# A mixed attention and FFN kernel: the first up product moved to VectorE, the router's V group moved forward, silu by tanh, one down phase

## Chip, cores, metric

One core of one Trainium2 chip. The metric is the device time of one execution in microseconds (us), median over several executions. In the profiles PE is TensorE's matmuls, PEld its weight loads, DVE VectorE, ACT ScalarE, POOL GpSimd, SP the engine that issues most transfers. A ratio is the mean time of one kernel's runs over the mean of the other's of the same rounds, so it isn't quite the ratio of the medians that are quoted.

## The reference, cut to what matters

```python
# x: [1, 2048, 1024] bf16, wqkv: [1024, 3072], w_gate, w_up: [1024, 3584], w_down: [3584, 1024]
g = sigmoid((x * gate_w).sum(-1, keepdims=True))
# A: linear attention over 32 heads of 32
q, k, v = split(x @ wqkv);  phi(t) = where(t > 0, t + 1, exp(t)) + 1e-6
kv = einsum("bhsd,bhse->bhde", phi(k), v);  z = phi(k).sum(s)
a = (phi(q) @ kv / (phi(q) . z + 1e-6)) @ wo
# B: one row of x, chosen by a router, goes through a gated FFN
r = x @ w_r;  idx = argmax(r)
y = (silu(x[idx] @ w_gate) * (x[idx] @ w_up)) @ w_down * sigmoid(r[idx])
b = x;  b[idx] += y
return g * a + (1 - g) * b
```

The 2048 rows are 16 tiles of 128. The FFN is for a single row, so its 22 MB of weights are each used once: they can be multiplied on TensorE (the row as weights, padded to 32 columns) or row by row on VectorE (weights times a per-partition scalar, added up), with a column sum at the end.

## The kernel before

K and V of each tile are made as "units" of eight matmuls into one of four PSUM buffers. ScalarE and VectorE empty a K or Q unit (relu, exp, then the phi on VectorE), ScalarE alone empties a V unit. V is cut in three groups; the third ("router group", `vb == 2`) also carries the columns of the router and of the gate.

```python
    ps_work = ctx.enter_context(tc.tile_pool(name="ps_work", bufs=4, space=PSUM))
    ...
    # start: K of tiles 2 and 3, then the router group of V of all tiles
    for t in (2, 3):
        kv_open(t)
        for nb in range(2): ...            # K units
    for t in range(NT):
        unit_V(t, 2)
    ...                                    # router: maximum, its row, load of that row of x
    for t in range(4, NT):                 # tiles: K, K, V, V, one or two Q; FFN steps between
        for nb in range(4):
            unit_KV(t, nb)
            ...
        for i in range(Q_PER_T[t]):
            unit_Q(*q_units.popleft())
            ffn_slot(t, 4 + i)
    unit_Q(*q_units.popleft())
    for t in range(NT - 4, NT):
        unit_KVACC(t)
    down_finish()                          # column sum of the down rows, row of x stored
    gates()
    unit_Q(*q_units.popleft())
    unit_Q(*q_units.popleft())
    ...
    ph1.close()                            # gives back the pools of the first phase
    ...
    tmpb = ctx.enter_context(tc.tile_pool(name="tmpb", bufs=2))
    ps_den = ctx.enter_context(tc.tile_pool(name="ps_den", bufs=3, space=PSUM))
```

The end of the down phase, and the first user of memory that `ph1.close()` gives back:

```python
    def down_finish():
        ps = ps_ffn.tile([P, 256], F32, tag="f", name="yps")
        ...                                                    # 4 column sums on TensorE
        brow = rt.tile([P, 256], BF, name="brow")              # rt is a pool of the first phase
        dve.scalar_tensor_tensor(brow[:], ps[:], sig[:, 0:1], xsel4[:], op0=ALU.mult, op1=ALU.add)
        nc.gpsimd.dma_start(out=xp[bass.ds(nonlocal_idx[0], 1), :]..., in_=brow[0:128:32, :])

    def den_group(pair):
        dps = ps_den.tile([P, 512], F32, tag="d")
        ...                                                    # 16 matmuls
        dn = tmpb.tile([P, 512], F32, tag="dn")                # tmpb is a pool of the last phase
        act.activation(dn[:], dps[:], ACTF.Identity, bias=eps_t[:, 0:1])
        ...
```

## Time and profile before

| | before |
|---|---|
| time, us (median of 3) | 250.39 |
| span of the profiled run, us | 248.1 |
| first matmul of the unbroken stream, us | 7.28 |
| end of the matmuls on the chain of waits (eight small ones follow), us | 244.29 |
| TensorE without a matmul record between these two, us | 1.6 |
| VectorE busy | 65% |

The third to fifth rows say it all: from 7.28 on TensorE works without a break. (The 1.6 us are each stretch's length less TensorE's busy time in it, added up from 7.28 on.)

### The profile page before, as it was taken

The numbers are of one execution on the slowest core, as the hardware profiler recorded it, in microseconds if no ns is written. First come the engines' busy times: TensorE is split into PE (matmuls) and PEld (weight loads), VectorE is DVE, ScalarE is ACT, GpSimd is POOL, SyncE is SP. The second block draws the span as 40 slices with busy tenths as digits, with TensorE's granted clock in tenths as the row PEclk, the third lists the DMA queues.
The fourth block names the chain that finished last, engine by engine and source line by source line (L and its number), as shares of the span: only waits on it lengthen the run. The fifth ranks groups of instructions, "written<-read, shape, count | busy, mean of one in ns | idle before, by whom it ended". The sixth has DMA issues, their size and how long they took to land.

```text
span 248.1 us, 4887 instructions
## 1 busy us (share of the span) xinstructions
PE 241.3 (97%) x1925; PEld 123.8 (50%) x1947; DVE 162.4 (65%) x261; ACT 127.5 (51%) x215; POOL 51.9 (21%) x100
## 2 busy tenths in 40 slices
PE   8899999999999999999999999999999999999994
PEld 3446776654555554454655456444444444444442
DVE  0045112279993479996979972586878999953442
ACT  3087333356556265457266555568887633333210
POOL 6000000300000100000340000211666689940000
PEclk9999999999999999999999999999999999999999
DMA  6999998569963693899299973130000563455122
GB/s 186 309 261 214 232 389 274 172 192 355 344 213 85 191 312 96 263 321 340 99 294 314 439 266 130 47 107 1 0 3 12 170 223 129 167 169 152 62 85 85
DMA packets 46309, 47.76 MB, mean 193 GB/s; under 512 B 16776, under 2 KB 35472, under 8 KB 46224
## 3 DMA queue, kind: packets, MB, share of 16 engines
q1 hardware_dynamic: 45648, 46.28, 61.4%
q0 software_dynamic: 608, 1.19, 1.8%
q8 instruction: 15, 0.25, 0.4%
q14 instruction: 6, 0.05, 0.1%
q10 hardware_dynamic: 32, 0.00, 0.0%
HBM read 39.33 MB, written 8.39 MB: 192 GB/s over the span
## 4 chain that ended last, share of the span: by engine, by line
PE 84%; DVE 9%; DMA 4%; issue 1%; SPq 1%; DVEq 0%
PE ps L83 77%; DVE gacc L83 6%; PE first L83 3%; DMA wt<-in_B_w_down_dram 2%; DMA wkv<-in_A_wqkv_dram 2%; PE kvacc L83 2%; DVE eg L83 1%; DVE pk L83 1%; PE dps L83 1%; PE pm L83 1%; SPq L83 1%; PE gps L83 0%; DVE pq_all L83 0%; DVE ot L83 0%; DVE sg L83 0%
## 5 line engine op out<-in xcount | busy, mean ns | idle before, releaser
L83 PE MATMUL ps<-wkv,xT 128*128 128x352 bf16 (+2 forms) x604 | 106.4, 334 | 0.3
L83 PEld LDWEIGHTS <-xT 128*128 128x128 bf16 x640 | 62.3, 98 | 49.7 <-issue 0.9
L83 PE MATMUL ps<-xT,wq 128*128 128x512 bf16 x244 | 57.0, 379 | 1.0 <-issue 0.6
L83 ACT ACTIVATE u<-ps 128x512 f32<-128x512 f32 x60 | 35.8, 597 | 40.0 <-PE ps L83 38.1
L83 PE MATMUL ps<-m_sb,pq_all 128*128 128x512 bf16 (+2 forms) x259 | 55.3, 372 | 0.3
L83 ACT ACTIVATE e<-u 128x512 f32<-128x512 f32 x64 | 40.3, 630 | 2.0
L83 PEld LDWEIGHTS <-pq_all 128*128 128x128 bf16 x264 | 25.5, 98 | 30.2 <-issue 0.4
L655 POOL TENSOR_TENSOR pq_all<-pq_all,rb 128x512 bf16<-128x512 bf16 x32 | 36.5, 1161 | 14.4 <-DVE rb L83 13.9
L83 PEld LDWEIGHTS <-wq 128*128 128x128 bf16 x256 | 24.1, 98 | 28.7 <-issue 2.2
L83 DVE SCALAR_TENSOR_TENSOR gacc<-wt,hcol,gacc 128x1024 f32<-128x1024 bf16 x27 | 34.6, 1280 | 2.3 <-DMA wt<-in_B_w_down_dram 1.9
L83 DVE SCALAR_TENSOR_TENSOR ot<-ps,gate,xg 128x512 bf16<-128x512 f32 (+2 forms) x33 | 23.5, 721 | 15.1 <-PE ps L83 14.2
L83 DVE SCALAR_TENSOR_TENSOR pq_all<-ps,e 128x512 bf16<-128x512 f32 x32 | 21.8, 684 | 15.0 <-ACT e L83 14.9
L83 ACT ACTIVATE xg<-xt,omg 128x1024 f32<-128x1024 bf16 x16 | 18.1, 1145 | 25.9 <-DVE ot L83 25.9
L83 DVE SCALAR_TENSOR_TENSOR pk<-ps,e 128x512 bf16<-128x512 f32 x28 | 19.1, 687 | 8.1 <-ACT e L83 8.0
L83 DVE STREAM_SHUFFLE rb<-rdp 128x512 f32<-128x512 f32 x32 | 22.4, 726 | 0.0
L83 ACT CAST vt<-ps 128x352 bf16<-128x352 f32 x32 | 14.5, 453 | 13.9 <-PE ps L83 13.7
L213 POOL MEMSET vt<- 128x22 bf16 x16 | 3.0, 277 | 71.7 <-PE kvacc L83 71.2
L83 DVE SCALAR_TENSOR_TENSOR gacc<-wt,xs_f,gacc 128x2048 f32<-128x2048 bf16 x7 | 16.4, 2344 | 0.0
L83 ACT CAST vc<-ps 128x320 bf16<-128x320 f32 x16 | 6.8, 427 | 9.9 <-PE ps L83 9.9
L83 DVE COPY rg<-ps 128x2 f32<-128x2 f32 x16 | 2.5, 161 | 13.0 <-ACT vc L83 13.0
L355 POOL DMA_DIRECT2D xs<-in_A_x_dram x1 | 0.7, 711 | 41.8 <-DVE sig L83 41.8
L83 DVE SCALAR_TENSOR_TENSOR pk<-first,e 128x512 bf16<-128x512 f32 x4 | 2.8, 692 | 8.7 <-ACT e L83 8.7
(101 smaller groups left out, 101.0 us busy)
## 6 DMA issues: line engine op xcount, KB each, us to landing
wt<-in_B_w_down_dram SPq DMA_DIRECT2D x14, 512.0 KB, 5.2
wt<-in_B_w_gate_dram SPq DMA_DIRECT2D x8, 512.0 KB, 5.1
wt<-in_B_w_up_dram SPq DMA_DIRECT2D x8, 512.0 KB, 8.8
xt<-xp SPq DMA_DIRECT2D x16, 256.0 KB, 2.6
out_dram<-ot SPq DMA_DIRECT2D x15, 256.0 KB, 2.0
wt<-in_B_w_gate_dram SPq DMA_DIRECT2D x8, 384.0 KB, 7.0
wt<-in_B_w_up_dram SPq DMA_DIRECT2D x8, 384.0 KB, 7.0
wkv<-in_A_wqkv_dram SPq DMA_DIRECT2D x8, 256.0 KB, 5.3
```

What stands on the lines that cost most here:

```text
L83: inst = fn(*a, **k)
L213: nc.gpsimd.memset(vt_t[t][:, :, 32:33], 1.0)
L355: nc.gpsimd.dma_start(out=xs8[:], in_=x2d[bass.ds(idx_val, 1), :].rearrange("o (c p) -> (o c) p", p=P))
L655: nc.gpsimd.tensor_tensor(sl, sl, rb[:], op=ALU.mult)
```

## The change

The intent: take the 32 matmuls of the first half's up product off TensorE, which is full, and give them as eight rows to VectorE, which isn't. To make room there, silu drops two slow reciprocals for a tanh, the router is settled sooner, so that its rows can start sooner, and all down rows stand in one phase at the end. Cut to its core:

```diff
-Q_PER_T = {4: 2, 5: 1, 6: 1, 7: 2, 8: 1, 9: 1, 10: 2, 11: 1, 12: 1, 13: 1, 14: 1, 15: 0}
+Q_PER_T = {4: 2, 5: 1, 6: 1, 7: 2, 8: 2, 9: 1, 10: 2, 11: 1, 12: 1, 13: 1, 14: 1, 15: 1}
-GATE_STEPS = {...}  # gate rows in tiles 4 to 7
+REDUCE_AFTER = {(6, 3): 0, (9, 4): 1}
+ROW_STEPS = {...}   # gate rows in tiles 3 to 5, up rows in tiles 6 to 9
-DOWN_STEPS = {8: ..., 15: (1, 1, 1)}
+DOWN_STEPS = {10: (0, 0, 0, 1, 1, 1), 11: (1, 1, 1, 1, 1), ... 15: (1, 1, 1, 1, 1)}
     ...
     for c in range(1, KC):
         load_k(c)
+    sp.dma_start(out=wkv[:, :, v_cut : 2 * D], ...)            # router group of V
     for t in (2, 3):
         sp.dma_start_transpose(out=xT[:, :, t * P : (t + 1) * P], ...)
-    sp.dma_start(out=wkv[:, :, v_cut : 2 * D], ...)
     ...
-    sp.dma_start(out=wq[:], in_=wqkv_v[:, :, 0:D])            # now behind the router's row
     ...
-    for t in (2, 3):
-        ...                                                    # K units of tiles 2 and 3
+    for t in range(3):
+        unit_V(t, 2, ps_t, "t")
+    unit_V(3, 2)
     ...
-    for t in range(NT):
+    for t in range(4, NT):
+        if t in (4, 12):
+            unit_KV(2, (t - 4) // 8)
         unit_V(t, 2)
     ...
     def finish_gate(half, ps, w):
-        act.activation(eg[:, 0:w], ps[:, 0:w], ACTF.Exp, scale=-1.0)
-        dve.tensor_scalar_add(eg[:, 0:w], eg[:, 0:w], 1.0)
-        dve.reciprocal(eg[:, 0:w], eg[:, 0:w])
-        dve.tensor_tensor(sg[:, 0:w], ps[:, 0:w], eg[:, 0:w], op=ALU.mult)
+        act.activation(sg, ps[:, 0:w], ACTF.Tanh, scale=0.5)
+        dve.scalar_tensor_tensor(sg, sg, 1.0, ps[:, 0:w], op0=ALU.add, op1=ALU.mult)
     ...
-        yield from g0
-        yield from u0
+        for wi, wmat in enumerate((B_w_gate, B_w_up)):
+            yield from half0_rows(wmat)
+            yield from gate_up(1, (wi,))
     ...
     for t in range(NT - 4, NT):
         unit_KVACC(t)
-    down_finish()
     gates()
     unit_Q(*q_units.popleft())
     unit_Q(*q_units.popleft())
+    down_finish()
```

More of the change, by code (lines that the diff above doesn't have):

```diff
@@ L32 @@
 N_WARM = 6
-Q_PER_T = {4: 2, 5: 1, 6: 1, 7: 2, 8: 1, 9: 1, 10: 2, 11: 1, 12: 1, 13: 1, 14: 1, 15: 0}
+Q_PER_T = {4: 2, 5: 1, 6: 1, 7: 2, 8: 2, 9: 1, 10: 2, 11: 1, 12: 1, 13: 1, 14: 1, 15: 1}
 VH = (11, 11, 10)
-GU_AFTER = {(7, 3): 8, (9, 3): 8, (11, 3): 8}
-KV_AFTER = {(7, 3): (4, 5, 6), (11, 3): (8, 9, 10)}
-KV_LAST = {(7, 3): 7, (11, 3): 11}
-FLUSH_AFTER = {(8, 3), (12, 1)}
-GATE_STEPS = {4: (0, 1, 0, 1, 0, 1), 5: (0, 0, 1, 0, 1), 6: (0, 1, 0, 1, 0), 7: (1,)}
+REDUCE_AFTER = {(6, 3): 0, (9, 4): 1}
+KV_AFTER = {(7, 3): (4, 5, 6, 7), (11, 3): (8, 9, 10, 11)}
+FLUSH_AFTER = {(10, 2)}
+ROW_STEPS = {4: (0, 1, 0, 1, 0, 1), 5: (0, 1, 0, 1, 1), 6: (0, 0, 0, 0, 1), 7: (0, 1, 1, 0, 1), 8: (0, 1, 0, 1, 1), 9: (1,)}
 M_AFTER = {3: (0, 0), 6: (0, 1), 9: (1, 0), 12: (1, 1)}
-DOWN_STEPS = {8: (0, 0, 0, 0, 1), 9: (1, 1, 1), 10: (0, 1, 1, 1, 1, 1), 11: (1, 1, 1), 12: (1, 1, 1, 1, 1), 13: (1, 1, 1, 0, 1), 14: (1, 1, 1, 0, 1), 15: (1, 1, 1)}
+DOWN_STEPS = {10: (0, 0, 0, 1, 1, 1), 11: (1, 1, 1, 1, 1), 12: (1, 1, 1, 1, 1), 13: (1, 1, 1, 1, 1), 14: (1, 1, 1, 1, 1), 15: (1, 1, 1, 1, 1)}
 FFN_DEPTH = 10
-NORM_PER_T = [3, 2, 0, 2, 2, 2, 2, 2, 2, 2, 2, 0, 0, 0, 0, 0]
+NORM_PER_T = [3, 3, 0, 2, 2, 2, 2, 2, 2, 2, 2, 1, 0, 0, 0, 0]
 @with_exitstack
@@ L76, with in_order @@
     strict = [True]
-    def in_order(engine, names):
+    strict_dve = [False]
+    def in_order(engine, names, own=(False,)):
         last = [None]
@@ L83, in call @@
                 inst = fn(*a, **k)
-                if last[0] is not None and strict[0]:
+                if last[0] is not None and (strict[0] or own[0]):
                     tc.add_manual_dep(inst.ins, last[0].ins.name, NOSYNC, reason="program order on this engine")
@@ L94 @@
     dve = in_order(nc.vector, ["memset", "tensor_copy", "tensor_scalar", "tensor_scalar_add", "tensor_tensor", "scalar_tensor_tensor",
-                               "reciprocal", "max", "max_index", "tensor_reduce", "stream_shuffle"])
+                               "reciprocal", "max", "max_index", "tensor_reduce", "stream_shuffle"], strict_dve)
     sp = in_order(nc.sync, ["dma_start", "dma_start_transpose"])
@@ L140 @@
         load_k(c)
+    v_cut = D + 32 * (VH[0] + VH[1])
+    sp.dma_start(out=wkv[:, :, v_cut : 2 * D], in_=wqkv_v[:, :, D + v_cut : 3 * D])
     for t in (2, 3):
         sp.dma_start_transpose(out=xT[:, :, t * P : (t + 1) * P], in_=x2d[t * P : (t + 1) * P, :])
-    v_cut = D + 32 * (VH[0] + VH[1])
-    sp.dma_start(out=wkv[:, :, v_cut : 2 * D], in_=wqkv_v[:, :, D + v_cut : 3 * D])
     for g4 in range(1, 4):
@@ L221, in kv_evac, with unit_V @@
         phi_dve(ps[:], phi_exp(ps[:]), pk_t[t][:, 512 * nb : 512 * nb + 512])
-    def unit_V(t, vb):
+    def unit_V(t, vb, pool=ps_work, tag="w"):
         h0, nh = sum(VH[:vb]), VH[vb]
         n = 32 * nh + (2 if vb == 2 else 0)
-        ps = ps_work.tile([P, 512], F32, tag="w")
+        ps = pool.tile([P, 512], F32, tag=tag)
         for c in range(KC):
@@ L292 @@
         phi_evac(first[1][nb][:], pk_t[1][:, 512 * nb : 512 * nb + 512])
-    for t in (2, 3):
-        kv_open(t)
-        for nb in range(2):
-            pool, tag = (ps_t, "t") if t == 2 else (ps_work, "w")
-            ps = pool.tile([P, 512], F32, tag=tag)
-            kv_mm(ps, t, nb, 0, KC)
-            kv_evac(ps, t, nb)
+    for t in range(3):
+        unit_V(t, 2, ps_t, "t")
+    unit_V(3, 2)
     ps_t_cm.__exit__(None, None, None)
@@ L314 @@
     dve.tensor_copy(r_bf[:], rg[:, 0, :])
-    unit_V(0, 0)
+    unit_KV(3, 0)
     rps = ps_ffn.tile([16, P], BF, tag="f")
@@ L369 @@
     h_bf = [rt.tile([P, 512], BF, name=f"h_bf{i}") for i in range(2)]
-    sg = rt.tile([P, 512], F32)
+    sg_t = [rt.tile([P, 512], F32, name=f"sg{i}") for i in range(2)]
     ffn_state = {}
@@ L390, in finish_gate, with h_transpose @@
     def finish_gate(half, ps, w):
-        eg = tmp.tile([P, 512], F32, tag="ffn_e", bufs=1)
-        act.activation(eg[:, 0:w], ps[:, 0:w], ACTF.Exp, scale=-1.0)
-        dve.tensor_scalar_add(eg[:, 0:w], eg[:, 0:w], 1.0)
-        dve.reciprocal(eg[:, 0:w], eg[:, 0:w])
-        dve.tensor_tensor(sg[:, 0:w], ps[:, 0:w], eg[:, 0:w], op=ALU.mult)
-    def finish_up(half, ps, w):
-        dve.tensor_tensor(h_bf[half][:, 0:w], ps[:, 0:w], sg[:, 0:w], op=ALU.mult)
-        def h_transpose():
-            hps = ps_ffn.tile([P, 16], F32, tag="f")
-            nb = w // P
-            for b in range(nb):
-                pe.matmul(hps[:, 4 * b : 4 * b + 4], lhsT=h_bf[half][:, b * P : (b + 1) * P], rhs=sel4[:], start=True, stop=True)
-            dst = hcol[:].rearrange("p (j b) -> p j b", b=7)[:, :, 4 * half : 4 * half + nb]
-            src = hps[:, 0 : 4 * nb].rearrange("p (b j) -> p j b", j=4)
-            dve.tensor_copy(dst, src)
-        ffn_state["pending"] = h_transpose
+        sg = sg_t[half][:, 0:w]
+        act.activation(sg, ps[:, 0:w], ACTF.Tanh, scale=0.5)
+        dve.scalar_tensor_tensor(sg, sg, 1.0, ps[:, 0:w], op0=ALU.add, op1=ALU.mult)
+    def finish_up(half, ps, w):
+        dve.scalar_tensor_tensor(h_bf[half][:, 0:w], ps[:, 0:w], 0.5, sg_t[half][:, 0:w], op0=ALU.mult, op1=ALU.mult)
+    def h_transpose():
+        hps = ps_ffn.tile([P, 28], F32, tag="f")
+        for b in range(7):
+            half, col = b // 4, P * (b % 4)
+            pe.matmul(hps[:, 4 * b : 4 * b + 4], lhsT=h_bf[half][:, col : col + P], rhs=sel4[:], start=True, stop=True)
+        dve.tensor_copy(hcol[:].rearrange("p (j b) -> p j b", b=7), hps[:].rearrange("p (b j) -> p j b", j=4))
     def gate_up(half, which):
@@ L427, in compute, with half0_rows @@
                     if c == KC - 1:
-                        if half == 0:
-                            ffn_state["up0"] = lambda: finish_up(half, ps, w)
-                        else:
-                            (finish_gate, finish_up)[wi](half, ps, w)
+                        (finish_gate, finish_up)[wi](half, ps, w)
                 yield load, compute
-    def gate_rows():
+    def half0_rows(wmat):
         for c in range(KC):
             def load(c=c):
-                return gate_up_load(0, B_w_gate, c)
+                return gate_up_load(0, wmat, c)
             def compute(wt, c=c):
@@ L447, in gate_rows, with rows_reduce @@
             yield load, compute
-    def gate_reduce():
-        ps = ps_red.tile([P, 512], F32, name="gps")
+    def rows_reduce(wi):
+        ps = ps_red.tile([P, 512], F32, tag="red", name=f"red{wi}")
         for j in range(4):
@@ L453, in gate_reduce @@
                       start=True, stop=True, tile_position=(0, 32 * j))
-        finish_gate(0, ps, 512)
-        ffn_state["up0"]()
+        (finish_gate, finish_up)[wi](0, ps, 512)
     def down_rows():
@@ L497, in ffn_pieces @@
     def ffn_pieces():
-        g0, u0, gu, dn = gate_rows(), gate_up(0, (1,)), gate_up(1, (0, 1)), down_rows()
-        yield from g0
-        yield from u0
-        for n in (2, 4):
-            yield from islice(dn, n)
-            yield from islice(gu, 8)
-        yield from dn
+        for wi, wmat in enumerate((B_w_gate, B_w_up)):
+            yield from half0_rows(wmat)
+            yield from gate_up(1, (wi,))
+        yield from down_rows()
         yield from wo_pieces()
@@ L515, in ffn_prefetch @@
             inflight.append((nxt[0](), nxt[1]))
-    def ffn_flush():
-        pend = ffn_state.pop("pending", None)
-        if pend is not None:
-            pend()
     def ffn_step(n):
@@ L554 @@
     q_units = deque((g, j) for j in range(4) for g in range(NG))
-    for t in range(4):
-        for vb in range(2):
-            if (t, vb) != (0, 0):
-                unit_V(t, vb)
+    unit_KV(3, 1)
     ffn_prefetch(2)
@@ L565, with reduce_at @@
     ffn_prefetch(4)
+    strict_dve[0] = True
     router_part1()
-    first_after[5] = xsel_ld[0]
+    wq_ld = nc.sync.dma_start(out=wq[:], in_=wqkv_v[:, :, 0:D])
+    queue_order(wq_ld)
+    tc.add_manual_dep(wq_ld.ins, xsel_ld[0].ins.name, SYNC, reason="small transfers ahead of the weights")
     ffn_prefetch()
     for t in range(4):
+        for vb in range(2):
+            unit_V(t, vb)
+            if (t, vb) == (3, 0):
+                router_part2()
+            if t == 3:
+                ffn_step(1)
+    for t in range(4):
         unit_KVACC(t)
+    def reduce_at(t, i):
+        if (t, i) in REDUCE_AFTER:
+            rows_reduce(REDUCE_AFTER[(t, i)])
+            ffn_step(8)
     def ffn_slot(t, i):
-        gs, ds = GATE_STEPS.get(t, ()), DOWN_STEPS.get(t, ())
+        gs, ds = ROW_STEPS.get(t, ()), DOWN_STEPS.get(t, ())
         if i < len(gs):
@@ L581 @@
             unit_KV(t, nb)
-            if (t, nb) == (4, 0):
-                router_part2()
             for t0 in KV_AFTER.get((t, nb), ()):
                 unit_KVACC(t0)
-            ffn_step(GU_AFTER.get((t, nb), 0))
-            if (t, nb) == (7, 3):
-                gate_reduce()
-            if (t, nb) in KV_LAST:
-                unit_KVACC(KV_LAST[(t, nb)])
+            reduce_at(t, nb)
             if (t, nb) in FLUSH_AFTER:
-                ffn_flush()
+                h_transpose()
             ffn_slot(t, nb)
@@ L595 @@
             unit_Q(*q_units.popleft())
+            reduce_at(t, 4 + i)
             ffn_slot(t, 4 + i)
+    strict_dve[0] = False
     unit_Q(*q_units.popleft())
```

## The prediction

> **What bounds the kernel now.** I read the page's busy shares first, then the stretches by time, then the waits of TensorE, then single rows of the time line where the change cuts in. The shares and the clock:
>
> ```profile
> span 248.1 us, 4887 instructions
> PE 241.3 (97%) x1925; PEld 123.8 (50%) x1947; DVE 162.4 (65%) x261; ACT 127.5 (51%) x215; POOL 51.9 (21%) x100
> PEclk9999999999999999999999999999999999999999
> ```
>
> TensorE is 97% busy at full clock and VectorE 65%. A busy TensorE may still run below its peak, so I check by stretch (us, then busy time of PE, PEld, DVE, ACT, POOL, clock, DMA share, GB/s):
>
> ```profile
> 0.00:7.28 7.28, 5.51 (x29) 2.59 (x29) 1.02 (x3) 2.45 (x3) 3.96 (x39) 1.00 0.73 206
> 7.28:13.95 6.67, 6.62 (x30) 3.01 (x31) 0.00 (x0) 1.01 (x2) 0.00 (x0) 1.00 1.04 272
> 13.95:39.50 25.55, 25.55 (x170) 16.27 (x167) 8.65 (x27) 14.76 (x31) 0.00 (x0) 1.00 1.13 291
> ...
> 84.00:121.50 37.50, 37.33 (x352) 19.67 (x353) 33.63 (x37) 21.38 (x38) 0.65 (x4) 1.00 0.80 243
> ```
>
> From 7.28 on there is no stretch in which TensorE is not full. In the chain of waits 49 matmuls of 512 columns take 10.74 us, 0.219 each; 56 of 352 columns take 8.46, 0.151 each. For 84 to 121.5 the units between are worth 37.7 us at these rates, which is the whole stretch: although the chain of waits runs through VectorE there, TensorE loses nothing by it. TensorE's own waits, all of them:
>
> ```profile
> PE warm_ps L83 <- PEq L741: 1.0, 1, 1.0
> PE first L83 <- DMA wkv<-in_A_wqkv_dram: 0.7, 1, 0.7
> PE ps L83 <- issue: 0.6, 4, 0.2
> ```
>
> So the time is: 7.3 us of start, 237 us of matmuls end to end (7.28 to 244.29), 3.8 us of tail. **The only gains to be had are fewer TensorE microseconds; the only losses are new waits on TensorE.** Start (the first K chunk) and tail are not touched.
>
> **What the Trainium skill says.** (1) "TensorE: Matmul & The Clock Gate", Part 3 on packing small matmuls by row and column tiling: matmuls on different column strips run concurrently. The trace agrees: the up product of the first half is 32 matmuls of 512 columns that take 1.74 us, 54 ns each, a quarter of 219. So removing 32 of 1925 matmul records removes little. (2) "VectorE: DVE Perf Modes", the perf-mode tier table: a one-source tensor_scalar may reach a higher tier than a two-source tensor_tensor with fp32, for which it gives 2293 ns at 2048 elements. The trace has 1286 ns for the one-source row and 2344 for the accumulating rows, in line. (3) "ScalarE: Activation LUTs", Table sets: exp and tanh lie in one set, so tanh should bring no table load; the trace of before has one load (1283 ns), and the instruction list of the changed kernel has one too. (4) "DMA: Bandwidth & Descriptors", Latency and other measured facts: an effective 261 GB/s for a transposing DMA. In the trace the transposes of tiles 4 to 7 and 12 to 15 land at 21.4 and 29.3 us (below), 2 MB (tiles 8 to 15) in 7.9 us, 265 GB/s: it agrees.
>
> **Part 1: up product on VectorE.** What goes and what comes on TensorE:
>
> ```profile
> 79.95 0.91 PE kvacc L83 x96
> 80.86 1.74 PE ps L83 x32
> 82.61 0.85 PE gps L83 x7
> ```
>
> The middle piece (1.74 us) goes; a second column sum in fp32 like the third (0.85 us) comes. Net -0.89 us. The transposes of h are the same seven matmuls. On VectorE:
>
> ```profile
> L83 DVE SCALAR_TENSOR_TENSOR gacc<-wt,xs_f,gacc 128x2048 f32<-128x2048 bf16 x7 | 16.4, 2344 | 0.0
> L83 DVE RECIPROCAL eg<-eg 128x512 f32<-128x512 f32 x1 | 3.4, 3354 | 0.0
> L83 DVE RECIPROCAL eg<-eg 128x384 f32<-128x384 f32 x1 | 2.5, 2545 | 0.0
> L83 DVE TENSOR_SCALAR gacc<-wt,xs_f 128x2048 f32<-128x2048 bf16 x1 | 1.3, 1286 | 0.0
> ```
>
> Seven more rows of 2.344 and one of 1.286 are +17.7 us. Silu by tanh takes away both reciprocals (3.35 + 2.55) and both additions of one (0.43 + 0.35), -6.7 us; the fused multiplies replace plain ones of like size. Net +11.0 us: VectorE goes from 162.4 to about 173.4 us (70%).
>
> Does it still fit? Per token tile TensorE needs two K units (1.75 each), two V units (1.21 each) and the Q units (1.75 each): 7.7 us with one Q, 9.4 with two. VectorE's pitch is read from the time line of 93 to 104 us: a phi 0.60, a down row behind a phi 1.20, behind another row 1.30.
>
> - Tiles 4, 7 and 8 (two Q, three gate or up rows): 4 x 0.60 + 3 x 2.3 = 9.3 against 9.4 us. Tile 5 (one Q): 1.8 + 6.9 = 8.7 against 7.7, but tile 6, with one row, gives the time back, and the order has both K phis of a tile ahead of its rows.
> - The sums of the rows stand at the ends of tiles 6 and 9. Followed row by row, the last row ends within a few tenths of the time that TensorE arrives there. I count 0.1 us.
> - Tiles 12 to 15 (one Q, five down rows): 3 x (0.60 + 1.20) + 2 x 1.30 = 8.0 against 7.7 us. Before, tiles 13 to 15 had four, four and three rows. VectorE falls behind by 0.3 us a tile, some 1.2 us at the end. With four PSUM buffers for these units, I find the phi that must free the buffer of the next Q about 1 us ahead of its use in tile 15. The last sum of the down rows now stands behind three Q units, so the lag doesn't reach it. I count 0.
>
> **Part 2: the router group of V first.** Before, tiles 2 and 3 did their K units (7.0 us) at 13.95, then the 16 router units of V (1.09 us each). Now V of tiles 0 to 3 comes at 13.95, one K pair's first half follows, and tile 4's V. The work is the same, but the transposed x is wanted sooner: for tile 4 at 13.95 + 4 x 1.09 + 1.75 = 20.1 us instead of 25.3. It lands so (start and length of the issue; then the time to landing of that issue, and of the one for tiles 12 to 15):
>
> ```profile
> 11.97 5.82 SPq L83 DMA_TRANSPOSE xT<-in_A_x_dram  x1
> ...
> xT<-in_A_x_dram SPq DMA_TRANSPOSE x1, 9.4
> ...
> xT<-in_A_x_dram SPq DMA_TRANSPOSE x1, 6.5
> ```
>
> That is 11.97 + 9.4 = 21.4 us for tiles 4 to 7, and 22.79 + 6.5 = 29.3 for 12 to 15. The V chunk moves ahead of the small transposes, but the same bytes stand ahead of this one, and the DMA share is full, so I expect 20.5 to 21.3: **a new wait of about 0.7 us**. The next groups are wanted at about 25.2 and 31.4 us and should be there. The V chunk itself was issued at 11.34 and took 4.9 us; issued at about 6.0, it should land by about 13.5, just ahead of its use at 13.95.
>
> The router result comes some 1.8 us sooner (its transpose at about 37.7 instead of 39.5 us); the selected row of x took 10.5 us from there (39.5 to 50.0), so it lands at about 48.2, where TensorE arrives at about 48.0: 0.15 us. Wq now waits for that row: it used 28.5 to 39.7 us before, mostly behind other loads; 2 MB alone at the 389 GB/s that the page shows in its slice from 31 to 37 us are 5.4 us, so it lands near 56 against a first use at 56.5. I count 0.1.
>
> **Part 3: one down phase, two more Q units early, down sum last.** The work is the same. The 5.6 us DMA wait for down weights in the middle of the old chain disappears, which TensorE didn't feel. The last M product now stands directly ahead of the output stage; its copies have about 3 us, and are wanted in about 3: 0.1 us.
>
> **Sum.** -0.89 + 0.7 + 0.1 + 0.15 + 0.1 + 0.1 = +0.26 us: 250.39 + 0.26 = 250.6. As the schedule was visibly tuned around these edges, and each small wait counted can be zero, I take 250.3.
>
> **Rivals.**
> (a) *No new wait is felt*: the transposes land by 20.1. For it: in before the V chunk was mixed into them. Against it: the DMA is full up to there. Time: 250.4 - 0.9 = 249.5.
> (b) *VectorE becomes the bound of tiles 11 to 15*: if each row cost its mean duration without overlap (0.68 a phi, 1.28 a row), a tile would take 8.45 against 7.7, the lag would be 3 to 4 us by tile 15, and the Q units and the sum would wait some 1.5 us. Against it: the overlap is in the time line. Time: 252.
> (c) *Wq is late*: weights issued ahead of it and the row's landing push it by 2 us, straight onto the first Q unit. For it: it is 2 MB with half a microsecond of margin. Time: 252 to 252.5.
> (d) *The freed router time is worth a lot*: no. Nothing on TensorE waited for it before.
>
> **Range and chances.** The floor is 250.4 - 0.9 - 0.6 (the waits named issue), 248.9; (b) and (c) together make 253.5. Eight in ten: 249.0 to 252.2. Two per cent faster would be 245.4, for which TensorE has not the work to lose: 0.01. Two per cent slower is 255.4, which needs two of the rivals at their worst: 0.03. Within: 0.96.
>
> **What would show it.** TensorE busy near 240.4 us; VectorE near 173; the pair (column sums) twice at 0.85; a wait of V on the transposed x near 20 us of some 0.7; no wait of TensorE for VectorE over 0.5 us in tiles 11 to 15; the first Q unit without a wait on Wq; one table load. I am wrong if a wait on VectorE or on Wq of over 1 us stands among TensorE's waits, or if the start of the matmuls moves from 7.28.

## The result, and the profile after

253.44 us (median of 4 runs, 253.17 to 254.03) against 250.29 in the same rounds: ratio 1.0127, 95% interval 1.0101 to 1.0153. The same within 2%, but 3.1 us slower than predicted, and outside the predicted range.

The shares of the changed kernel:

```profile
span 251.8 us, 4856 instructions
PE 241.7 (96%) x1897; PEld 123.6 (49%) x1923; DVE 172.5 (69%) x264; ACT 127.5 (51%) x215; POOL 51.8 (21%) x100
```

VectorE came out as worked out (172.5 us against 173.4 predicted). 26 of TensorE's matmul records are missing here, so its sum is rough. Three of its stretches (start and end, length, then busy time of PE, PEld, DVE, ACT, POOL, clock, DMA share, GB/s):

```profile
13.40:36.95 23.55, 22.86 (x153) 14.67 (x152) 7.16 (x25) 12.40 (x27) 0.00 (x0) 1.00 1.05 246
...
124.50:163.60 39.10, 38.63 (x328) 20.02 (x336) 37.98 (x43) 22.64 (x40) 4.51 (x10) 1.00 0.60 199
163.60:191.20 27.60, 25.45 (x213) 10.95 (x210) 19.54 (x37) 20.71 (x39) 10.36 (x12) 1.00 0.11 35
```

The largest hole, 2.15 us, lies between 163.6 and 191.2, right behind the phase that was reordered, where the kernel before has 0.42 in a like stretch, all of it holes of missing records:

```profile
156.00:192.00 36.00, 35.58 (x266) 15.28 (x273) 27.18 (x56) 28.07 (x50) 15.08 (x16) 1.00 0.09 28
```

From the first matmul of the stream to the last, TensorE is without a record for 5.3 us in the changed kernel, 1.6 in the kernel before. TensorE's waits in the changed kernel, in order of size (us in total, times, longest):

```profile
PE pt L83 <- ACT dn L83: 1.8, 1, 1.8
...
PE ps L83 <- issue: 0.8, 5, 0.2
PE ps L83 <- DMA xT<-in_A_x_dram: 0.6, 1, 0.6
PE kvacc L83 <- issue: 0.4, 1, 0.4
PE ps L83 <- POOL pq_all L642: 0.3, 1, 0.3
PE ps L83 <- DMA wq<-in_A_wqkv_dram: 0.3, 1, 0.3
```

(The line left out is the warm-up's, 1.0 us in both kernels.) Not all of this is real. The profile of this run has 1897 matmul records, a later one of the same kernel (`after_again`) all 1923; that of the kernel before has 1925, with 1947 weight loads. In the chain of waits of this run, the last 51 us of matmuls come in pieces of 49 with a hole behind each:

```profile
210.88 0.05 issue
210.94 10.74 PE ps L83 x49
```

In that of `after_again` they are one piece:

```profile
196.40 51.49 PE ps L83 x240
```

So these holes are missing records. The five holes of 0.2 us named `issue` are of the same kind: no profile with all its records has them. The hole of 0.4 at `kvacc` isn't: all 128 matmuls of that group are there. Its cause the profile doesn't show, and no other profile has it.

Waits on xT and on Wq were in the prediction's list, and one at the output stage too, though for the copies of the last M product; here it is GpSimd's normalised `pq`. The first wasn't in the list: TensorE's product `pt` waits for ScalarE's `dn`. The chain of waits of the changed kernel around that place says why:

```profile
163.03 0.57 PE yps L83 x8
163.60 0.96 PE dps L83 x16
164.57 2.48 DMA xp<-brow
...
167.44 0.69 ACT dn L83
...
168.17 0.29 PE pt L83 x30
```

`dn` empties the denominators that `dps` made, which were there at 164.6; it starts at 167.4, when the store of `brow` has landed. The two have nothing to do with each other but memory: `brow` is in a pool of the first phase, `dn` in a pool of the last, and the second takes what the first gives back, so `dn` must wait until the store has read. (Which addresses overlap the profile doesn't show. The memsets of `rdp`, the first writes to the last pools' memory, wait for the store too, in both kernels: they start at 167.2 here and at 159.2 before.) And `pt` must wait for `dn`, because its four banks are the three of `ps_den` and one more, and `dps` holds one of the three. The time line of ScalarE in the kernel before has the same instruction without a wait, since there the store was issued at 157.4 and landed 1.7 us later, at 159.1, before `dps` was done (160.2):

```profile
160.38 0.67 ACT L83 ACTIVATE dn<-dps,eps_t 128x512 f32<-128x512 f32 x1
```

So the dependency isn't new. The change moved its release onto the path. Two theories for the 3 us, then. **Memory**: moving the down sum behind the Q units brings out the wait for `brow`'s store, and the smaller waits on transfers at the start make the rest. **Load**: VectorE, with 10 us more to do, runs late (it is 97% busy from 124.5 to 163.6), and what shows as waits is its delay.

### The profile page after: what moved, and what is told of

It reads as the page before. It is cut to its first block, busy times and chain, and to the rows that moved or that the text cites. A ratio compares the mean times of both kernels' runs of the same rounds, so it can differ in the third digit from the quotient of the medians.

```text
span 251.8 us, 4856 instructions
## 1 busy us (share of the span) xinstructions
PE 241.7 (96%) x1897; PEld 123.6 (49%) x1923; DVE 172.5 (69%) x264; ACT 127.5 (51%) x215; POOL 51.8 (21%) x100
## 4 chain that ended last, share of the span: by engine, by line
PE 77%; DMA 11%; SPq 3%; DVE 2%; issue 2%; ACT 1%; POOL 0%; POOLq 0%; DVEq 0%; ACTq 0%
PE ps L83 73%; DMA wq<-in_A_wqkv_dram 4%; DMA xT<-in_A_x_dram 3%; SPq L83 3%; DMA wkv<-in_A_wqkv_dram 2%; PE kvacc L83 2%; DMA xsel<-in_A_x_dram 1%; DMA xp<-brow 1%; PE red L83 1%; PE dps L83 1%; DVE pq_all L83 1%; SPq L537 1%; DMA c<-cand 1%; DVE rb L83 1%; ACT e L83 1%
## 5 line engine op out<-in xcount | busy, mean ns | idle before, releaser
L83 DVE SCALAR_TENSOR_TENSOR gacc<-wt,xs_f,gacc 128x2048 f32<-128x2048 bf16 x14 | 32.8, 2345 | 0.2
L83 DVE RECIPROCAL rd<-dn 128x512 f32<-128x512 f32 x2 | 6.7, 3353 | 3.2 <-POOL rdp L603 3.2
```

Source lines behind the costliest of these rows:

```text
L83: inst = fn(*a, **k)
```

## The experiments

### e1: memory of its own for brow

```diff
-        brow = rt.tile([P, 256], BF, name="brow")
+        brow = keep.tile([P, 256], BF, name="brow")
```

> The changed kernel, with the row that the down sum stores (brow) in memory that nothing reuses. Theory: the largest loss (TensorE's 1.8 us wait of pt for ACT dn) comes from dn taking memory that brow gives back, so that it must wait for brow's store to land, and the down sum is now so late that this landing is on the path. Then the wait goes and the time falls by 1.5 to 2.1 us, to about 251.5. Rival: VectorE's lag behind the down rows delays everything at that place; then the time stays within 0.4 us of 253.4.

252.09 us (251.82 to 252.54), ratio to before 1.0079 (1.0053 to 1.0105), against 1.0127 and, on another chip, 1.0171 of the changed kernel: 1.2 to 2.3 us less. (The changed kernel was not run in the rounds of e1 to e4, so these comparisons go by the ratios to the kernel before.) TensorE's wait at `pt` is gone; those on xT and Wq are longer in this profile (1.0 and 0.7 instead of 0.6 and 0.3), which hides some of the gain. ScalarE's time line:

```profile
164.74 0.69 ACT L83 ACTIVATE dn<-dps,eps_t 128x512 f32<-128x512 f32 x1 [0.26 <-PE dps L83]
```

`dn` now waits for `dps` alone. VectorE has exactly the same work as in the changed kernel, so its load isn't the cause of this wait. The time line says the same: in the changed kernel VectorE began `brow` at 163.80, 0.2 us after the down sum (163.60). The memory theory holds.

### e2: the kernel before, with the down sum last

```diff
-    down_finish()
     gates()
     unit_Q(*q_units.popleft())
     unit_Q(*q_units.popleft())
+    down_finish()
```

> The kernel before, with one thing of the change alone: the down sum moved behind the last two Q units. VectorE isn't late there in this kernel. Theory of the memory that brow gives back: dn must wait for brow's store, TensorE waits 1.0 to 2.0 us at pt, and the time is about 251.3 to 252.3 against 250.3. Rival (VectorE's lag is the cause): no change, 250.3 within 0.4.

250.99 us against 250.07, ratio 1.003 (1.0005 to 1.0055). That one move, with an unhurried VectorE, brings out the wait:

```profile
PE pt L83 <- ACT dn L83: 0.8, 1, 0.8
```

The direction is that of the theory; the sizes are under what was expected, the wait (0.8 instead of 1.0 to 2.0) and the time (0.9 us more by the medians, 250.99 where 251.3 to 252.3 stood). The store takes 1.6 us from issue to landing in this profile, and 2.5 in that of the changed kernel (2.3 in its second profile, where `pt` waits 1.6). The wait differs as the landing does. Why the same 2 KB store lands later in one program than in another, these runs don't show.

### e3: both K units of tile 2 ahead of V of tile 4

```diff
-        if t in (4, 12):
-            unit_KV(2, (t - 4) // 8)
+        if t == 4:
+            unit_KV(2, 0)
+            unit_KV(2, 1)
```

> The changed kernel, with both K units of tile 2 ahead of V of tile 4 (before one of the two), so that the transposed x of tile 4 is wanted 1.75 us later. Theory: TensorE's wait of some 0.65 us near 20 us goes and comes back nowhere, so the time falls by 0.5 to 0.8 us, to about 252.8. Rival: the transposes as a whole are late, and the wait moves to tiles 8 or 12; then under 0.2 us.

252.73 us (252.24 to 254.32), ratio 1.0107 (1.0074 to 1.014). By the ratios it is 0.5 to 1.6 us faster than the changed kernel, by the profiled spans 0.8 (251.0 against 251.8). The intervals of the ratios overlap, so the time line has to decide. TensorE's time line at the start, in the changed kernel:

```profile
20.20 16.75 PE L83 MATMUL ps<-wkv,xT 128*128 128x322 bf16 x111 [0.64 <-DMA xT<-in_A_x_dram]
```

and in e3, where the hole is gone and nothing has taken its place:

```profile
13.61 22.84 PE L83 MATMUL ps<-wkv,xT 128*128 128x322 bf16 x150
```

### e4: Wq at its old place in the queue

```diff
+    sp.dma_start(out=wq[:], in_=wqkv_v[:, :, 0:D])       # behind the V loads, as before
     ...
-    wq_ld = nc.sync.dma_start(out=wq[:], in_=wqkv_v[:, :, 0:D])
-    ...                                                  # behind the router's row
+    first_after[5] = xsel_ld[0]                          # as before: a weight load waits for that row
```

> The changed kernel, with the load of Wq at its old place in the queue, ahead of the first gate weights. Theory: the wait of the first Q unit (0.3 us) goes and the time falls by 0.2 to 0.4 us, to about 253.1. Rival: the router's small transfers then run beside it and the selected row comes later, so that TensorE waits at the transposes of that row, up to 1 us; then it is slower than the changed kernel.

254.69 us, ratio 1.0187 (1.0155 to 1.022): slower than the changed kernel by 0.4 to 1.5 us by the ratios to before, though their intervals overlap (two of the six runs, the profiled one among them, had a clock of 0.993). The theory failed: the wait on Wq is gone, and a larger one has come, of the rival's kind and beyond the 1 us that the rival allowed:

```profile
PE xs_ps L83 <- DMA xs<-in_A_x_dram: 1.9, 1, 1.9
```

With 2 MB more in flight, the router's tiny candidate transfers take 4.1 us instead of 1.7 to land (medians), and the load of the row is issued at 46.5 instead of 43.7. Of that delay 2.4 us are the transfers; 0.5 us are due to the stream of matmuls, which ran that much later in this profile. Putting Wq behind the row was a sound choice in the changed kernel; it needs finer dosing.

### e5: the up product of the first half back on TensorE

```diff
     ...   # REDUCE_AFTER and ROW_STEPS without the up rows
-        for wi, wmat in enumerate((B_w_gate, B_w_up)):
-            yield from half0_rows(wmat)
-            yield from gate_up(1, (wi,))
+        yield from half0_rows(B_w_gate)
+        yield from gate_up(1, (0,))
+        yield from gate_up(0, (1,))
+        yield from gate_up(1, (1,))
```

> The changed kernel unchanged, on the chip of the three that follow, as their base: 1.0127 of the kernel before, within 0.003, and TensorE's wait at pt again 1.6 to 2.0 us, the one on the transposed x 0.4 to 1.0.

> The changed kernel with one part undone: the up product of the first half on TensorE again (32 matmuls, no second column sum; VectorE loses eight rows, 17.7 us). Theory: part 1 is by itself a gain of the size predicted, so TensorE gets 1.74 more and 0.85 to 1.0 less, and its second wait on the row sums (0.4) goes: 0.3 to 0.9 us slower than the changed kernel, with the wait at pt unchanged. Rival: VectorE's extra load is what delays the changed kernel; then it is at least 1 us faster.

The changed kernel again: 253.95 us, ratio 1.0171 (1.0136 to 1.0206; two of its six runs had a clock of 0.993), a little outside what was expected; its waits as expected (1.6 at `pt`, 0.9 on xT). e5: 253.84, ratio 1.0149 (1.0128 to 1.017), so no slower: the 0.3 to 0.9 us expected did not show. The comparison of times is spoilt: in e5's profile `brow`'s store landed in 1.7 us instead of 2.3 and the wait at `pt` was 0.9 instead of 1.6, while the one on xT was 1.4 instead of 0.9. The time lines still tell what TensorE's extra work costs: from the first Q unit to the first `pt`, where it waits for nothing in either profile, e5 takes 110.5 us (56.93 to 167.44) and the changed kernel 109.5 (57.20 to 166.72). And 17 us less on VectorE (155.9 against 172.5) win nothing: the load theory expected at least 1 us.

### e6 and e7: the waits taken away together

e6 is e1 and e3 with a quarter of Wq loaded early and the rest behind the router's row. e7 also moves each row sum back by one unit and begins normalising one Q unit earlier:

```diff
 # e6
+    sp.dma_start(out=wq[:, :, 0:256], in_=wqkv_v[:, :, 0:256])
-    wq_ld = nc.sync.dma_start(out=wq[:], in_=wqkv_v[:, :, 0:D])
+    wq_ld = nc.sync.dma_start(out=wq[:, :, 256:D], in_=wqkv_v[:, :, 256:D])
 # e7
-REDUCE_AFTER = {(6, 3): 0, (9, 4): 1}
+REDUCE_AFTER = {(6, 4): 0, (10, 0): 1}
-        if i >= 4:
+        if i >= 3:
             norm_step(1)
```

> The changed kernel with own memory for brow, both K units of tile 2 ahead of V of tile 4, and the first quarter of Wq loaded early with the rest behind the router's row. Theory: the three waits (pt 1.8, transposed x 0.7 to 1.0, Wq 0.3 to 0.7) are separate and add up; together 2.6 to 3.2 us faster than the changed kernel, about 250.4, level with the kernel before. Rival: they hide behind each other; then under 2.2. A quarter of Wq is 512 KB ahead of the gate weights, so the row could come 1 us later; then a wait at xs_ps shows.

> e6 with each row sum one unit later and the normalising begun one Q unit earlier. Theory: the two waits on the row sums (0.3 and 0.4) and the one of the output stage on normalised pq (0.3) go: 0.5 to 1.0 us faster than e6, about 249.6, which is 0.2 to 0.4 per cent faster than the kernel before. Rival: another wait takes their place (h needed at the transposes; the shuffles waiting for rdp); then within 0.2 us of e6.

e6: 250.38 us (249.7 to 250.62), 3.6 less than the changed kernel on the same chip (2.6 to 3.2 were expected), ratio to before 1.0007 (0.9988 to 1.0026). The three waits (1.6, 0.9 and 0.4 in the changed kernel's profile of these rounds) add up; none was hiding another. A wait of 0.5 us for the router's row shows, as feared. e7: 249.66 (249.31 to 250.26), ratio 0.9981 (0.9963 to 0.9999): 0.7 faster than e6. The wait on pq is gone from its list. Those on the row sums were waits of weight loads only, and they did not go: two loads idle 0.7 us before `red` in e6 (put down to VectorE's `gacc`) and 0.8 in e7 (put down to `issue`), and the pair of sums takes 0.99 us in the chain of the changed kernel as in that of e8. Moving the sums won nothing that the traces show.

### e8 and e9: the row one unit later; part 1 weighed

e8 is e7 with the transposes of the router's row behind the last V unit of tile 3 instead of ahead of it. e9 is e7 with the edit of e5.

> e7 unchanged, on another chip, as the base of the two that follow: 0.998 of the kernel before, within 0.002; its one large wait is 0.7 us for the router's row at xs_ps.

> e7 with the transposes of the router's row one V unit later on TensorE (and the first two gate rows with it). Theory: the wait at xs_ps (0.7 us) is hidden by that unit of 1.2 us and comes back nowhere, as the sums of the rows have been moved back by a unit: 0.4 to 0.7 us faster than e7, about 249.1. Rival: the gate rows are now later, so the first row sum waits: within 0.2 us of e7.

> e7 with the up product of the first half on TensorE again, so that part 1 is weighed where no other large wait stands. Theory: TensorE gets 1.74 us more and 0.85 to 1.0 less, 0.7 to 0.9 us slower than e7, about 250.4. Rival: with less to do VectorE frees buffers sooner and the time stays within 0.3 us of e7, so that the predicted gain of part 1 was none.

| kernel | median, us | ratio to before (95%) |
|---|---|---|
| before | 250.04 | |
| e7 again | 249.79 | 0.9993 (0.9956 to 1.0029) |
| e8 | 249.20 | 0.9952 (0.9923 to 0.998) |
| e9 | 250.61 | 1.0008 (0.9979 to 1.0036) |

e7 again missed its expectation: the wait of 0.7 us at xs_ps, there in e7's first profile, isn't in the list of this one. e8 is 0.6 us faster than e7, the size that was expected, and faster than both original kernels. That the gain is that wait, hidden, isn't shown: the base of this comparison didn't have it in its profile, and the intervals of the two ratios overlap. All that TensorE still waits for in e8 is the start and 0.2 us on the transposed x:

```profile
PE warm_ps L83 <- PEq L729: 1.0, 1, 1.0
PE ps L83 <- DMA xT<-in_A_x_dram: 0.2, 1, 0.2
```

e9 is 0.82 us slower than e7 by the medians, as the theory has it; by the ratios it is 0.4, and their intervals overlap, so the time alone doesn't settle it. The work does. TensorE's groups in e9 (the up product, and one row sum), then in e8 (two row sums):

```profile
L83 PE MATMUL ps<-wt,xs_pad 128*32 128x512 bf16 x32 | 1.9, 380 | 0.0
L83 PE MATMUL red<-gacc,ones_f 128*32 128x512 f32 x8 | 1.1, 604 | 0.0
```

```profile
L83 PE MATMUL red<-gacc,ones_f 128*32 128x512 f32 x16 | 2.1, 605 | 0.0
```

1.9 us go and 1.0 come. And from the first Q unit to the first `pt`, without a wait in either, e9 takes 110.5 us (56.24 to 166.76) and e7 again 109.4 (55.28 to 164.66). Both pairs, e5's and this one, give part 1 a gain of about 1 us on TensorE.

## Why the prediction was wrong, point by point

| term | predicted, us | the changed kernel |
|---|---|---|
| TensorE's work | -0.89 | -0.75 (1.74 less 0.99 in the chains of waits); -1.0 and -1.1 by e5 and e9 |
| wait on the transposed x | +0.7 | 0.64 and 0.94 in two profiles (landing at 20.2 and 21.0, 20.5 to 21.3 predicted) |
| wait on Wq | +0.1 | 0.28 and 0.4 |
| wait for the router's row | +0.15 | none; 0.3 on weight loads in the second profile |
| wait on the row sums | +0.1 | none of matmuls; 0.7 on weight loads, as much in e7 with the sums moved |
| VectorE in tiles 11 to 15 | 0 | no wait of TensorE on it |
| the output stage (copies of M) | +0.1 | none on those copies; 0.3 on pq |
| part 3, the down sum last | 0 | 1.8 and 1.6 at `pt` |

**The step that failed** is part 3: "The work is the same", and in part 1: "The last sum of the down rows now stands behind three Q units, so the lag doesn't reach it. I count 0." I asked whether the sum would come late for what it needs, and not who needs what it holds. Its output row's memory is taken over by `dn`: 1.8 us of wait, which e1 takes away, and of which e2 brings out 0.8 in the kernel before. None of the rivals named it.

**Wq and the output stage** were sized too small. That Wq landed at 56.14, against the 56 that I gave, is luck: my own terms, 48.2 for the row and 5.4 us for 2 MB, make 53.6. The row landed at 47.0, and Wq took 9.1 us, with gate weights issued just before and behind it. What failed is the margin of half a microsecond. The first Q unit was ready at 55.9 in this profile and at 56.8 in the second, where Wq landed at 57.2. The start of the matmul stream, which I had taken as fixed at 7.28, was 6.83 and 7.30 in the two, so it doesn't explain the wait. It lies between 6.2 and 7.5 in the profiles, whatever the kernel; as a sign of being wrong it was worthless. At the output stage I counted the copies of M; what TensorE waited for was pq.

**Each wait costs more than its line.** A matmul's record is 379 ns long at a pitch of 219 ns, so the first 0.16 us of a wait are still "busy". I had both numbers before me and added up lines without them. The sum, from the two profiles: of the 5.3 us without a record, 1.9 are holes of missing records (21 of some 0.05 us, five of 0.16), as are all the 1.6 of the kernel before. The 0.6 us named `issue` that stood in my floor were never there to be had. The other 3.4 us are five waits: 1.76 at `pt`, 0.64, 0.28 and 0.32 on xT, Wq and pq, 0.40 at `kvacc`. With the hidden 0.16 for each that makes some 4.1. Less 0.75 to 1.1 of work, less 0.45 for the earlier start, plus 0.4 in the tail, it is 3.0 to 3.3; the spans differ by 3.7. The tail belongs to the change and not to the run: 3.80 us behind the matmuls in the profiles of before and e2, 4.2 in both of the changed kernel. Its cause wasn't looked for, and the last few tenths stay open.

**What was right**: no gain to be had but TensorE's own, and its size (0.75 to 1.1 us against 0.89); the wait on the transposed x near 20 us, its size and its cause (e3); VectorE's 173 us, its overlap, and that it bounds nothing (rival b falls, by e5 too); one table load for exp and tanh (a single one of 1283 ns in the changed kernel as well). Rival (c), a late Wq, was true in kind at 0.3 us. One reading was loose: the 265 GB/s beside the skill's 261 come from the spacing of two landings. In that stretch (21.4 to 29.3 us) the core moved 242 GB/s in all. And "DMA: Bandwidth & Descriptors" gives the 261 for a non-contiguous middle dimension only, and more for the contiguous case.

## What to carry to other kernels

When a step is moved later, look not only at what it waits for but at what waits for its memory: a small store at the end of a phase holds its buffer until it lands, and the first writer of the next phase may sit on that address. A buffer of 512 bytes per partition in a pool that isn't reused bought 1.2 to 2.3 us here. In a kernel whose main engine is full, count each new edge as a wait plus the part of it that the engine's records cover, and dose a large transfer instead of moving it whole: in e6, a quarter of Wq early and the rest late took its wait away, at 0.5 us for the router's row. Before reading small idle times, compare the number of matmul records with that of a complete profile.

## What the Trainium skill lacked or had wrong

- "VectorE: DVE Perf Modes", perf-mode tier table: it has no row for a scalar_tensor_tensor. Here one of 2048 elements, bf16 weights times a per-partition scalar added to fp32, took 2345 ns (14 of them in the changed kernel), 2% more than the 2293 ns of its tensor_tensor row for fp32.
- "Perfetto Trace Analysis", Identifying the Most-Contended Engine: it warns that matmul busy time is no measure of distance to the roofline; it lacks what that does to waits. Here the first 0.16 us of each wait stood under busy (379 ns records at a pitch of 219).
- No page that I read says that a store's source buffer, handed to the next phase, holds up its first writer until the landing: 1.6 to 2.5 us for a 2 KB store here, of which 0.8 to 1.8 fell on TensorE.
